# A square root on ScalarE for the first tile, and a new order of work at the start of a norm, mixer and attention kernel

## The chip, the cores and the metric

The kernel runs on one core of one Trainium2 chip. The metric is the device time of one execution in microseconds (us).

## The reference, cut to what matters

```python
def _layernorm(x, axis=-1, eps=1e-05):
    m = jnp.mean(x, axis=axis, keepdims=True)
    v = jnp.var(x, axis=axis, keepdims=True)
    return (x - m) / jnp.sqrt(v + eps)
# x: (1, 2048, 1024) bf16
xn = _layernorm(x)
return x + _A_ref(xn, mem0, Wq, Wk, Wv, Wo, seg_len) + _B_ref(xn, w1, w2, w3, w4)
# _B_ref begins with:  h = gelu(layernorm(xn) @ w1)
```

Everything waits for the norm of x. The kernel cuts the 2048 rows into 16 tiles of 128 rows and starts with branch B: it normalizes a tile twice in one step, transposes it, and multiplies it by w1 (1024 x 1024). The long rest (99% of the time) is dense matrix work.

Of the kernel before, what the change touches and what calls it, by code (L numbers as in the profile page):

```python
# [16 lines left out]
F32 = mybir.dt.float32  # L17
I32 = mybir.dt.int32
ALU = mybir.AluOpType
ACTF = mybir.ActivationFunctionType  # L20
# [3 lines left out]
P = 128  # L24
S = 2048
D = 1024
KT = D // P
# [9 lines left out]
EPS = 1e-5  # L37
# [40 lines left out]
def kernel(  # L78
# [16 lines left out]
    nc = tc.nc  # L95
# [46 lines left out]
    ones_f = cpool.tile([P, 1], F32)  # L142
# [4 lines left out]
    epsa = cpool.tile([P, 2], F32)  # L147
# [46 lines left out]
    with tc.manual_schedule(engines={mybir.EngineType.PE, mybir.EngineType.SP, mybir.EngineType.Pool}), ExitStack() as actx:  # L194
# [6 lines left out]
        with ExitStack() as bctx:  # L201
# [13 lines left out]
            with ExitStack() as hctx:  # L215
# [7 lines left out]
                with ExitStack() as p0:  # L223
                    big = p0.enter_context(tc.tile_pool(name="p0big", bufs=1))
# [4 lines left out]
                    xts = {}  # L229
# [18 lines left out]
                    stats = {}  # L248

                    def norm_stats(n, part=None):  # L250

                        if n >= NT:
                            return
                        xt = xts[n]
                        if n not in stats:
                            stats[n] = [ring.tile(shape, F32, tag=tag, bufs=6, name=f"{tag}{n}") for tag, shape in (("st", [P, 2, 6]), ("mv", [P, 2]), ("ab", [P, 2]), ("rr", [P, 2]), ("nm2", [P, 1]))]
                        st, mv, ab, rr, nm2 = stats[n]
                        if part in (None, 0):
                            nc.vector.bn_stats(st[:, 0, :], xt[:, 0:512])
                        if part == 0:  # L260
                            return
                        nc.vector.bn_stats(st[:, 1, :], xt[:, 512:1024])
                        nc.vector.bn_aggr(mv[:], st[:])
                        nc.vector.scalar_tensor_tensor(ab[:], epsm[:], mv[:, 1:2], epsa[:], op0=ALU.mult, op1=ALU.add)
                        nc.gpsimd.tensor_tensor(rr[:], ab[:], neghalf[:], op=ALU.pow)
                        if n >= NPE:
                            nc.gpsimd.tensor_scalar(nm2[:], mv[:, 0:1], rr[:, 1:2], -1.0, op0=ALU.mult, op1=ALU.mult)

                    def norm2(n, xn2T, jj):
                        st, mv, ab, rr, nm2 = stats[n]  # L270
                        xn2 = ring.tile([P, D], BF16, tag="xn2")
                        if n < NPE:
                            for c in (slice(0, 512), slice(512, 1024)) if n == 0 else (slice(0, 1024),):
                                nc.vector.tensor_scalar(xn2[:, c], xts[n][:, c], mv[:, 0:1], rr[:, 1:2], op0=ALU.subtract, op1=ALU.mult)
                        else:
                            nc.scalar.activation(xn2[:], xts[n][:], ACTF.Identity, bias=nm2[:], scale=rr[:, 1:2])
                            nc.sync.dma_start_transpose(xn2T[:, jj], xn2[:])
                        return xn2
# [11 lines left out]
                    def transposes(xn2, xn2T, jj, half, shared=False):  # L290
                        ps = psum0.tile([P, 4, P], F32, tag="tr")
                        for k in range(4):
                            nc.tensor.matmul(ps[:, k, :], xn2[:, (half * 4 + k) * P:(half * 4 + k + 1) * P], ident[:], start=True, stop=True)
                        if shared:
                            nc.scalar.copy(xn2T[:, jj, half * 4:half * 4 + 2, :], ps[:, 0:2])
                            nc.vector.tensor_copy(xn2T[:, jj, half * 4 + 2:half * 4 + 4, :], ps[:, 2:4])
                        else:
                            nc.scalar.copy(xn2T[:, jj, half * 4:half * 4 + 4, :], ps[:])

                    def stage1_k(xn2T):  # L300

                        pss = [psum.tile([P, 4, P], F32, tag="mm", bufs=4, name=f"ps{i}") for i in range(2)]
                        for k in range(KT):
                            if k == KT - 1:
                                tr(1, 0)
                                tr(1, 1)
                            for co in range(KT):
                                nc.tensor.matmul(pss[co // 4][:, co % 4, :], w1_sb[:, k, co * P:(co + 1) * P], xn2T[:, 0, k, :],
                                                 start=(k == 0 and co % 4 == 0), stop=(k == KT - 1), skip_group_check=True)
                        for i in range(2):  # L310
                            nc.scalar.activation(hTB[:, 4 * i:4 * i + 4, 2:2 + P], pss[i][:], ACTF.Gelu_apprx_tanh)
# [12 lines left out]
                    def xn2T_tile():  # L324
                        return ring.tile([P, 2, KT, P], BF16, tag="xn2T", name="xn2T")
# [2 lines left out]
                    wz = big.tile([P, 512], BF16)  # L328
                    nc.vector.memset(wz[:], 0.0)
                    gtab = big.tile([P, 1], F32)  # L330
                    nc.scalar.activation(gtab[:], ones_f[:], ACTF.Gelu_apprx_tanh)

                    ps = psum.tile([P, 512], F32, tag="mm", bufs=4, name="warm")
                    for i in range(12):
# [3 lines left out]
                    def norm2_of(n):  # L338
                        if n % 2 == 0:
                            tiles2[n] = xn2T_tile()  # L340
                        xn2s[n] = norm2(n, tiles2[n - n % 2], n % 2)

                    def tr(n, half, shared=False):
                        transposes(xn2s[n], tiles2[n - n % 2], n % 2, half, shared)

                    norm_stats(0)
                    norm_stats(1, 0)
                    norm2_of(0)
                    tr(0, 0, True)
                    tr(0, 1, True)  # L350
                    norm_stats(1, 1)
                    nc.gpsimd.memset(hTB[:, :, 0:2], 0.0)
                    nc.gpsimd.memset(hTB[:, :, S + 2:S + 4], 0.0)
                    load_consts(4)
                    for n in range(1, NPE):
                        if n > 1:
                            norm_stats(n + 1, 0)
                        norm2_of(n)
                        norm_stats(n + 1, 1 if n > 1 else None)
                        if n > 1:  # L360
                            norm1(n - 2)
                        if n == 1:
                            stage1_k(tiles2[0])
                        elif n < 4:
                            stage1(n - 1, 1, tiles2[(n - 1) // 2 * 2], {4: [lambda n=n: tr(n, 0)], 5: [lambda n=n: tr(n, 1)]}, (n - 1) % 2)
# [20 lines left out]
                with ExitStack() as p2:  # L386
                    ring = p2.enter_context(tc.tile_pool(name="p2ring", bufs=4))
                    for n in range(NT):
                        x1 = ring.tile([P, D], F32, tag="x1")
                        st = ring.tile([P, 2, 6], F32, tag="st")  # L390
                        for ch in range(2):
                            ps = psum.tile([P, 512], F32, tag="mm", bufs=4)
# [5 lines left out]
                        mv = ring.tile([P, 2], F32, tag="mv")  # L398
# [14 lines left out]
            with ExitStack() as p3:  # L413
                psum3 = p3.enter_context(tc.tile_pool(name="psum3", bufs=2, space=PSUM))
                h3T = p3.enter_context(tc.tile_pool(name="p3h", bufs=1)).tile([P, FT, 512], BF16)
                big = p3.enter_context(tc.tile_pool(name="p3big", bufs=1))
# [115 lines left out]
                for tb in range(4):  # L532
                    depth = 1 if tb < 2 else 2
                    for f in range(FT):
                        ps = psum.tile([P, 512], F32, tag="mm", bufs=4)
# [15 lines left out]
                    for j in range(4):  # L551
                        n = tb * 4 + j
# [7 lines left out]
                        for ch in range(2):  # L560
                            ps = psum.tile([P, 512], F32, tag="mm", bufs=4)
# [21 lines left out]
            for hg in range(8):  # L583
# [6 lines left out]
                for m4 in range(4):  # L590
                    Vs = vsp.tile([P, 4, 512], BF16, tag="Vs")
                    for j in range(4):
                        ps = psum.tile([P, 512], F32, tag="mm", bufs=4)
# [180 lines left out]
        for gi_, group in enumerate(groups):  # L774
# [3 lines left out]
            for hg in range(8):  # L778
# [24 lines left out]
                step = 8 * sum(8 * (B["nb"] / 2400 + 0.0025) for B in Bs) / len(work)  # L803
                step = (step * len(work) + 0.36 * len(work)) / len(work)
# [50 lines left out]
        for i in range(2):  # L855
            ps = psum.tile([P, 512], F32, tag="mm", bufs=4)
# [34 lines left out]
    with tc.If(cond > 0):  # L891
        with ExitStack() as fctx:
# [18 lines left out]
            with tc.For_i(0, NSEG, 1) as i:  # L911
# [6 lines left out]
                for hg in range(8):  # L918
# [8 lines left out]
                    ps = fps.tile([P, 4, L], F32, tag="mm")  # L927
# [4 lines left out]
                    ps = fps.tile([P, 4, L], F32, tag="mm")  # L932
# [4 lines left out]
                    ps = fps.tile([P, 512], F32, tag="mm")  # L937
# [33 lines left out]
                for ch in range(2):  # L971
                    ps = fps.tile([P, 512], F32, tag="op")
# [47 lines left out]
```

## The kernel before: the parts that the change touches

```python
load_x(0)                                  # 256 KB each, on the SyncE queue
for c in range(4):                         # w1 in four pieces of 512 KB, two k each
    nc.sync.dma_start(w1_sb[:, 2*c:2*c+2, :], w1_v[:, 2*c:2*c+2, :])
    if c == 0:
        load_x(1)
for n in range(2, 7):
    load_x(n)
# ... w2 and more x tiles

def norm_stats(n, part=None):              # VectorE statistics, then the power on POOL
    # ...
    if part in (None, 0):
        nc.vector.bn_stats(st[:, 0, :], xt[:, 0:512])
    if part == 0:
        return
    nc.vector.bn_stats(st[:, 1, :], xt[:, 512:1024])
    nc.vector.bn_aggr(mv[:], st[:])
    nc.vector.scalar_tensor_tensor(ab[:], epsm[:], mv[:, 1:2], epsa[:], op0=ALU.mult, op1=ALU.add)
    nc.gpsimd.tensor_tensor(rr[:], ab[:], neghalf[:], op=ALU.pow)      # 1/sqrt

def transposes(xn2, xn2T, jj, half, shared=False):
    # four matmuls with the identity into ps, then the copy to SBUF:
    if shared:                                                          # tile 0 only
        nc.scalar.copy(...first two blocks...)
        nc.vector.tensor_copy(...last two blocks...)
    else:
        nc.scalar.copy(...all four...)

def stage1_k(xn2T):                        # tile 0, k outermost, so it follows w1's pieces
    for k in range(KT):                    # KT = 8
        if k == KT - 1:
            tr(1, 0)                       # tile 1's transposes
            tr(1, 1)
        for co in range(KT):
            nc.tensor.matmul(...)          # 128x128x128
    # ... Gelu

# 12 warm-up matmuls of 128x512, then:
norm_stats(0)
norm_stats(1, 0)
norm2_of(0)                                # xn2 = (x - mean) * rr, in two halves
tr(0, 0, True)
tr(0, 1, True)
norm_stats(1, 1)
# ... then for n = 1, 2, ...: norm, statistics of n + 1, stage 1
```

The stage-1 loop of tile 0 is called "the first stage" below, that of tile 1 "the second stage". Tile 2's transposes come in the middle of the second stage.

## Time and profile before

| | before |
|---|---|
| median when the prediction was made (3 executions) | 1516.68 us (1515.07 to 1517.80) |
| median of 6 executions, the first 3 among them | 1515.14 us (1514.63 to 1517.80) |
| span of the profiled execution | 1512.7 us |
| first norm on VectorE | 6.58 us |
| first transpose on TensorE | 7.03 us |
| first matmul of the first stage | 7.89 us |
| tile 2's transposes | 14.71 us |

The busy shares and the chain of waits of the profile's page of before:

```profile
PE 1502.8 (99%) x9778; PEld 807.9 (53%) x9850; DVE 545.2 (36%) x1138; ACT 504.1 (33%) x1142; POOL 178.9 (12%) x248
...
PE 98%; DMA 1%; issue 0%; ACT 0%; DVE 0%; SPq 0%
```

PE is TensorE, DVE VectorE, ACT ScalarE, POOL GpSimd, and a lower case q behind an engine means its queue of DMA issues. TensorE is the limit nearly everywhere. What TensorE waited for (engine, line, releaser: us in total, number of times, longest):

```profile
...
PE ps L293 <- DVE xn L274: 0.4, 1, 0.4
PE psO L706 <- DMA PT<-Pn: 0.2, 1, 0.2
```

So there is little to win, and nearly all of it lies in the first 13 us. The profile models the end of a matmul with some 0.16 us of draining, so this view understates or omits short waits. Below, "waits of PE" are taken from the starts of consecutive matmuls in the trace, less their normal pitch (56 ns for 128 columns at full clock).

The timeline of before, cut (start, busy us, engine, line, operation, out<-in, count, and in brackets the idle time and what ended it):

```profile
1.38 5.30 PE L335 MATMUL warm<-wz 128*128 128x512 bf16 x12 [1.38 <-DVE wz L329]
...
5.34 0.72 POOL L265 TENSOR_TENSOR rr<-ab,neghalf 128x2 f32<-128x2 f32 x1 [2.73 <-DVE ab L264]
...
5.97 0.69 DVE L259 BATCH_NORM_STATS2 st<-xt 128x6 f32<-128x512 bf16 x1 [0.72 <-DMA xt<-in_A_x_dram]
6.58 0.72 DVE L274 TENSOR_SCALAR xn<-xt,mv,rr 128x512 bf16<-128x512 bf16 x2
...
7.03 0.72 PE L293 MATMUL ps<-c_ident_sb,xn 128*128 128x128 bf16 x8 [0.35 <-DVE xn L274]
...
7.89 3.29 PE L308 MATMUL ps<-xn2T,w_sb 128*128 128x128 bf16 x56
...
11.00 0.69 DVE L259 BATCH_NORM_STATS2 st<-xt 128x6 f32<-128x512 bf16 x1
...
11.14 0.62 PE L293 MATMUL ps<-c_ident_sb,xn 128*128 128x128 bf16 x8
...
12.22 2.66 PE L318 MATMUL ps<-xn2T,w_sb 128*128 128x128 bf16 x40
...
14.71 0.39 PE L293 MATMUL ps<-c_ident_sb,xn 128*128 128x128 bf16 x4
```

POOL is done with the power at 6.06, but VectorE has just begun half of tile 1's statistics (5.97), because x tile 1 landed at 5.94; so the norm of tile 0 runs only at 6.58. TensorE waits 0.13 us before 11.14 for tile 1's norm, 0.17 before 12.22 and 0.27 at the fifth matmul of that group (12.70) for the copies of tile 1. Tile 2's statistics start at 11.00, behind tile 1's norm and without waiting for x tile 2, which the trace shows landing at 10.69. Tile 2's transposes (14.71) wait for nothing.

### The profile page before, as it was taken

The page shows a single profiled execution, that of the slowest core. Times are in us where ns is not written, and L with a number is a line of the kernel's source. Part 1 is how long each engine was busy: PE and PEld are TensorE (multiplying, and loading weights), DVE is VectorE, ACT ScalarE, POOL GpSimd, SP SyncE. Part 2 cuts the span into 40 slices and gives each one's busy share as a digit, 9 for nine tenths or more (in the row PEclk, how much of TensorE's full clock was granted, in tenths as well). Part 3 has the DMA queues.
Part 4 walks back from the last instruction along what each step waited for, and adds up shares of the span by engine and source line. Part 5 has one row for each costly group of instructions (what it writes and reads, how often), then busy time and mean ns, then how long its engine had stood idle before and what let it go on. Part 6 is the DMA issues. An engine that isn't in the chain of part 4 may idle for free.

```text
span 1512.7 us, 24295 instructions
## 1 busy us (share of the span) xinstructions
PE 1502.8 (99%) x9778; PEld 807.9 (53%) x9850; DVE 545.2 (36%) x1138; ACT 504.1 (33%) x1142; POOL 178.9 (12%) x248
## 2 busy tenths in 40 slices
PE   9999999999999999999999999999999999999998
PEld 7844444445444444444466645664665455545555
DVE  8382230100020122222246624651564166516642
ACT  6533203013012011111256614650663266416630
POOL 5231020211111231100000010001000100010001
PEclk9999999999999999999999999999999999999999
DMA  8699762353345887632399947992998299818811
GB/s 295 147 255 334 218 176 91 137 202 112 125 163 145 196 274 253 208 120 84 126 245 242 246 124 183 245 238 71 239 248 203 73 227 224 216 60 212 190 47 52
DMA packets 303539, 274.11 MB, mean 181 GB/s; under 512 B 153926, under 2 KB 270184, under 8 KB 303424
## 3 DMA queue, kind: packets, MB, share of 16 engines
q1 hardware_dynamic: 281248, 189.92, 50.5%
q0 software_dynamic: 22032, 82.54, 15.8%
q8 instruction: 79, 1.29, 0.4%
q14 instruction: 36, 0.29, 0.1%
q10 hardware_dynamic: 144, 0.07, 0.0%
HBM read 190.93 MB, written 46.14 MB: 157 GB/s over the span
## 4 chain that ended last, share of the span: by engine, by line
PE 98%; DMA 1%; issue 0%; ACT 0%; DVE 0%; SPq 0%
PE ps L667 30%; PE pso L725 15%; PE ps L595 15%; PE ps L537 13%; PE ps L563 13%; PE ps L395 4%; PE ps L318 3%; PE psS L682 2%; PE psO L706 2%; PE ps L860 1%; PE ps L487 1%; PE gps L466 0%; PE ps L452 0%; DMA PT<-Pn 0%; DMA xt<-in_A_x_dram 0%
## 5 line engine op out<-in xcount | busy, mean ns | idle before, releaser
L667 PE MATMUL ps<-hTb,wt 128*128 128x396 bf16 (+2 forms) x2528 | 497.5, 343 | 0.0
L667 PEld LDWEIGHTS <-wt 128*128 128x128 bf16 x2528 | 232.8, 98 | 166.4
L595 PE MATMUL ps<-wt,xT 128*128 128x512 bf16 x1003 | 220.1, 379 | 1.1
L725 PE MATMUL pso<-wo_sb,oX 128*128 128x512 bf16 (+1 forms) x972 | 209.3, 372 | 1.1
L537 PE MATMUL ps<-xn3T,w_sb 128*128 128x512 bf16 x896 | 196.2, 379 | 0.0
L563 PE MATMUL ps<-w_sb,h3T 128*128 128x512 bf16 x873 | 194.3, 379 | 1.2
L595 PEld LDWEIGHTS <-xT 128*128 128x128 bf16 x1024 | 100.2, 98 | 120.8
L538 ACT ACTIVATE h3T<-ps 128x512 bf16<-128x512 f32 x112 | 66.8, 597 | 290.4 <-PE ps L537 289.5
L725 PEld LDWEIGHTS <-oX 128*128 128x128 bf16 x992 | 96.1, 98 | 106.5
L673 ACT CAST KT<-ps 128x462 bf16<-128x462 f32 (+2 forms) x160 | 81.9, 512 | 191.0 <-PE ps L667 189.2
L563 PEld LDWEIGHTS <-h3T 128*128 128x128 bf16 x896 | 87.0, 98 | 103.3
L537 PEld LDWEIGHTS <-w_sb 128*128 128x128 bf16 x896 | 86.6, 98 | 102.1
L688 DVE TENSOR_REDUCE sums<-sm 99x4 f32<-99x396 f32 (+2 forms) x176 | 97.6, 555 | 113.2 <-ACT sm L686 113.2
L675 ACT ACTIVATE QT<-ps 128x462 bf16<-128x462 f32 (+2 forms) x160 | 83.9, 525 | 113.1 <-PE ps L667 101.5
L597 ACT CAST Vs<-ps 128x512 bf16<-128x512 f32 x64 | 37.5, 586 | 233.2 <-PE ps L595 174.9
L684 DVE TENSOR_TENSOR sm<-psS,c_mask_reg_sb 99x396 f32<-99x396 f32 x152 | 86.7, 570 | 76.9 <-PE psS L682 76.9
L686 ACT ACTIVATE sm<-sm 99x396 f32<-99x396 f32 (+2 forms) x176 | 92.7, 527 | 59.0 <-DVE sm L684 54.1
L601 DVE CAST Vs<-ps 128x512 bf16<-128x512 f32 x64 | 44.3, 692 | 170.0 <-PE ps L595 160.4
L694 DVE TENSOR_TENSOR Pn<-sm,rs 99x396 bf16<-99x396 f32 (+2 forms) x176 | 98.9, 562 | 7.3 <-DMA PT<-Pn 1.2
L564 DVE TENSOR_TENSOR R<-ps,R 128x512 f32<-128x512 f32 x32 | 21.9, 690 | 180.5 <-PE ps L563 166.3
L732 POOL DMA_DIRECT2D out_dram<-ot x30 | 16.3, 545 | 587.2 <-DVE ot L731 581.4
L731 DVE TENSOR_TENSOR ot<-pso,Rt 128x512 bf16<-128x512 f32 (+1 forms) x33 | 22.3, 675 | 171.7 <-PE pso L725 166.3
(124 smaller groups left out, 1071.5 us busy)
## 6 DMA issues: line engine op xcount, KB each, us to landing
wt<-in_A_Wq_dram SPq DMA_DIRECT2D x76, 512.0 KB
wt<-in_A_Wk_dram SPq DMA_DIRECT2D x76, 512.0 KB
wt<-in_A_Wv_dram POOLq DMA_DIRECT2D x24, 1024.0 KB, 6.6
V_scratch<-Vs SPq DMA_DIRECT2D x32, 512.0 KB
V<-V_scratch SPq DMA_DIRECT2D x40, 384.0 KB
R_scratch<-x POOLq DMA_DIRECT2D x16, 512.0 KB, 5.1
R<-R_scratch SPq DMA_DIRECT2D x16, 512.0 KB
R_scratch<-R POOLq DMA_DIRECT2D x16, 512.0 KB, 3.6
```

Source lines behind the costliest of these rows:

```text
L537: nc.tensor.matmul(ps[:].rearrange("p (n t) -> p n t", t=P), w3_sb[:, k, f * P:(f + 1) * P], xn3T[tb][:, :, k, :], start=(k == 0), stop=(k ...
L538: nc.scalar.activation(h3T[:, f, :], ps[:], ACTF.Gelu_apprx_tanh)
L563: nc.tensor.matmul(ps[:], h3T[:, f, j * P:(j + 1) * P], w4_sb[:, f, ch * 512:(ch + 1) * 512], start=(f == 0), stop=(f == FT - 1))
L595: nc.tensor.matmul(ps[:], xT[:, m4 * 4 + j, k, :], wv[:, k, :], start=(k == 0), stop=(k == KT - 1))
L667: nc.tensor.matmul(ps[:, :nb] if flat else ps[:, :nb].rearrange("p (t c) -> p t c", t=nt), w[:, k, hh * P:(hh + 1) * P], B["rhs"](k), star ...
L673: nc.scalar.copy(o, i)
L675: nc.scalar.mul(o, i, scale)
L684: nc.vector.tensor_tensor(sm[:T, :, :T], S3, t["mask"][:].unsqueeze(1).to_broadcast((T, 4, T)), op=ALU.add)
L686: nc.scalar.activation(e[:T, :, :T], sm[:T, :, :T], ACTF.Exp, scale=LN2)
L688: nc.vector.tensor_reduce(ss, e[:T, :, :T], axis=AX.X, op=ALU.add)
L694: nc.vector.tensor_tensor(Pn[:T, :, :T], e[:T, :, :T], rs[:T, :].unsqueeze(2).to_broadcast((T, 4, T)), op=ALU.mult)
L725: nc.tensor.matmul(self.ps[:, :self.w], self.oX[0][:, h, self.oX[1] + self.gl * P:self.oX[1] + (self.gl + 1) * P], wo_sb[:, h, self.cc], s ...
```

## The change

The intent: get tile 0's scale from a square root on ScalarE and a reciprocal on VectorE, not from POOL; norm tile 0 before any statistics of tile 1; leave tile 0's copies to ScalarE alone; and issue tile 1's transposes one k sooner, so that two steps of matmuls hide their copies. The price is a second load of ScalarE's activation table, as the square root and Gelu belong to different sets (the changed trace has that load at 5.48 us, between the two).

```diff
@@ norm_stats
                         nc.vector.bn_aggr(mv[:], st[:])
+                        if n == 0:
+                            return
+                        scales(n)
+                    def scales(n):
                         nc.vector.scalar_tensor_tensor(ab[:], epsm[:], mv[:, 1:2], epsa[:], ...)
                         nc.gpsimd.tensor_tensor(rr[:], ab[:], neghalf[:], op=ALU.pow)
@@ norm2
-  ... mv[:, 0:1], rr[:, 1:2], ...
+  ... mv[:, 0:1], sd0[:, 1:2] if n == 0 else rr[:, 1:2], ...
@@ transposes
-                        if shared:
-                            nc.scalar.copy(...first two...)
-                            nc.vector.tensor_copy(...last two...)
-                        else:
-                            nc.scalar.copy(...all four...)
+                        step = 2 if shared else 4
+                        for i in range(0, 4, step):
+                            nc.scalar.copy(...blocks i to i + step...)
@@ stage1_k
-                            if k == KT - 1:
+                            if k == KT - 2:
                                 tr(1, 0)
@@ start
-                    nc.scalar.activation(gtab[:], ones_f[:], ACTF.Gelu_apprx_tanh)
+                    nc.scalar.activation(gtab[:], ones_f[:], ACTF.Sqrt)
 ...
                     norm_stats(0)
-                    norm_stats(1, 0)
+                    sd0 = big.tile([P, 2], F32)
+                    nc.scalar.activation(sd0[:, 0:1], stats[0][1][:, 1:2], ACTF.Sqrt, bias=epsa[:, 1:2], scale=1.0 + EPS)
+                    nc.vector.reciprocal(sd0[:, 1:2], sd0[:, 0:1])
                     norm2_of(0)
+                    scales(0)
+                    nc.scalar.activation(gtab[:], ones_f[:], ACTF.Gelu_apprx_tanh)
                     tr(0, 0, True)
                     tr(0, 1, True)
-                    norm_stats(1, 1)
+                    norm_stats(1)
```

No DMA is added, removed or reordered.

More of the change, by code (lines that the diff above doesn't have):

```diff
@@ L263, in norm_stats @@
                         nc.vector.bn_aggr(mv[:], st[:])
+                        if n == 0:
+                            return
+                        scales(n)
+                    def scales(n):
+                        st, mv, ab, rr, nm2 = stats[n]
                         nc.vector.scalar_tensor_tensor(ab[:], epsm[:], mv[:, 1:2], epsa[:], op0=ALU.mult, op1=ALU.add)
@@ L273, in norm2 @@
                             for c in (slice(0, 512), slice(512, 1024)) if n == 0 else (slice(0, 1024),):
-                                nc.vector.tensor_scalar(xn2[:, c], xts[n][:, c], mv[:, 0:1], rr[:, 1:2], op0=ALU.subtract, op1=ALU.mult)
+                                nc.vector.tensor_scalar(xn2[:, c], xts[n][:, c], mv[:, 0:1], sd0[:, 1:2] if n == 0 else rr[:, 1:2], op0=ALU.subtract, op1=ALU.mult)
                         else:
@@ L293, in transposes @@
                             nc.tensor.matmul(ps[:, k, :], xn2[:, (half * 4 + k) * P:(half * 4 + k + 1) * P], ident[:], start=True, stop=True)
-                        if shared:
-                            nc.scalar.copy(xn2T[:, jj, half * 4:half * 4 + 2, :], ps[:, 0:2])
-                            nc.vector.tensor_copy(xn2T[:, jj, half * 4 + 2:half * 4 + 4, :], ps[:, 2:4])
-                        else:
-                            nc.scalar.copy(xn2T[:, jj, half * 4:half * 4 + 4, :], ps[:])
+                        step = 2 if shared else 4
+                        for i in range(0, 4, step):
+                            nc.scalar.copy(xn2T[:, jj, half * 4 + i:half * 4 + i + step, :], ps[:, i:i + step])
                     def stage1_k(xn2T):
```

## The prediction

> **What bounds the kernel now.** TensorE: busy 1502.8 of 1512.7 us (first table of the page); the chain of waits is 98% PE. By the starts of consecutive matmuls in the trace, PE truly waits about 0.3 us after 26 us (once, for PT at 797 us). The change touches the first 15 us, so it can win only the few waits there.
>
> **The start, from the timeline of before.** The first x tile lands at 3.44; statistics to 4.99; ab 5.03; POOL's power 5.34 to 6.06; but VectorE has meanwhile begun 0.69 us of statistics of tile 1 (5.97), so the first norm's halves run at 6.58 and 6.89. The twelve warm-up matmuls (427 ns apart) end their issue near 6.47; the first transpose starts at 7.03, its copies at 7.47, stage 1's first matmul at 7.89. PE waits 0.13 us before tile 1's transposes (11.15), 0.17 before the second stage (12.22) and 0.27 in it (12.70, second copy). Tile 2's transposes start at 14.71 without a wait.
>
> **Costs and moves.**
> - Off tile 0's path go ab (0.22), the power (0.72, plus hand-overs) and half statistics of tile 1. On come a 128x1 ScalarE op (about 0.23, after the 0.20 of the table-warming one) and a 128x1 VectorE reciprocal (about 0.2): xn2's first half at about 6.0 in place of 6.98.
> - PE can't use all of that: the warm-up holds it to about 6.47, and the first transposes then run at half clock (until about 7 us). They end near 7.1 in place of 7.43: 0.35 us won.
> - ScalarE loads a table again behind the root. In the Trainium skill, "ScalarE: Activation LUTs", section "What ACT_TABLE_LOAD costs", a switch is 1283 ns plus a drain of about 1380. This trace shows 1283 ns twice, each time with the next activation 11 ns later: no further drain. So 5.29 to 6.79 with the activation behind it, free before the copies at 7.1.
> - Copies: four of 372 ns on ScalarE, 0.32 apart; stage 1 takes 0.45 us for each k, two per copy: nothing waits. VectorE loses 0.76 us of copies.
> - Tile 1's norm is done near 9.65 in place of 11.09. Transposes one step (0.45 us) sooner hide their copies behind two k steps: the waits 0.13 + 0.17 + 0.27 go.
>
> Sum 0.92 us. But tile 2's x lands only at 10.69. From its statistics to its norm's end the trace shows 3.2 us, so xn2 of tile 2 is ready near 13.95, and PE arrives near 13.8: 0.15-0.2 given back. Net gain **about 0.75 us**, 0.05%.
>
> **Time.** 1516.68 minus 0.75, and the four known executions of before average 0.6 below the median: **1515.6 us**, range 1513.6 to 1517.6. Faster by over 2% 0.003, within 2% 0.994, slower 0.003. Three runs of before spread over 2.7 us, so the gain will barely show in the times, only in the trace.
>
> **If right, the profile shows** the first norm at about 5.6; the first transpose near 6.5, directly behind the warm-up, at doubled pitch until the clock rises; stage 1's first matmul near 7.5; a table load at 5.3 of 1.28 us; no wait around tile 1's transposes; the second stage starting near 11.55; a new short wait of PE for xn2 before tile 2's transposes, which start near 13.95 in place of 14.71; later PE work shifted by 0.7-0.8 us.
>
> **What would make it wrong.** A drain around the second table load (copies at 8 us: a loss of about 0.2). The clock rising at another moment. x tiles or w1 pieces landing earlier or later (w1's last lands at 10.01, needed at 10.65). A later wait that takes the shift back.

## The result, and the profile after

| | before | changed |
|---|---|---|
| median of 6 executions | 1515.14 us (1514.63 to 1517.80) | 1515.41 us (1514.31 to 1516.37) |
| span of the profiled execution | 1512.7 us | 1513.3 us |
| first norm | 6.58 | 5.70 |
| first transpose | 7.03 | 6.17 |
| first matmul of the first stage | 7.89 | 7.29 |
| statistics of tile 2 start | 11.00 | 11.62 |
| tile 2's transposes | 14.71 | 14.85 |

The ratio is 0.9998, with a 95% interval of 0.9985 to 1.0011: the same. That interval is about 4 us wide around a predicted effect of 0.75 us, so the times cannot judge the prediction; the trace has to.

The page of the changed kernel (its lines are numbered 4 to 8 higher from the start section on; L299 is L293 of before, L312 is L308, L322 is L318, L280 is L274):

```profile
PE 1506.1 (100%) x9850; PEld 807.6 (53%) x9850; DVE 544.3 (36%) x1137; ACT 506.4 (33%) x1147; POOL 178.9 (12%) x248
...
PE 98%; DMA 1%; ACT 0%; DVE 0%; SPq 0%; issue 0%; POOL 0%
```

PE's busy time is not comparable here: the trace of before lacks 72 matmul records (9778 against 9850). What TensorE waited for in the changed kernel:

```profile
...
PE ps L299 <- DVE xn L280: 0.6, 1, 0.6
PE ps L312 <- ACT xn2T L302: 0.4, 1, 0.4
PE psO L714 <- DMA PT<-Pn: 0.3, 1, 0.3
PE ps L312 <- DMA w_sb<-in_B_w_dram: 0.3, 1, 0.3
```

The wait for xn (VectorE's norm) is no longer that of tile 0 but one in front of tile 2's transposes, and a wait for a piece of w1 is new. The timeline of the changed kernel, cut as that of before:

```profile
1.38 4.65 PE L339 MATMUL warm<-wz 128*128 128x512 bf16 x12 [1.38 <-DVE wz L333]
...
5.17 0.30 ACT L352 ACTIVATE sd<-mv,epsa 128x1 f32<-128x1 f32 x1 [2.92 <-DVE mv L263]
5.48 1.28 ACT L356 ACT_TABLE_LOAD   x1
...
5.70 0.74 DVE L280 TENSOR_SCALAR xn<-xt,mv,sd 128x512 bf16<-128x512 bf16 x2
...
6.17 0.72 PE L299 MATMUL ps<-c_ident_sb,xn 128*128 128x128 bf16 x8
...
6.78 0.20 ACT L356 ACTIVATE gtab<-ones_f 128x1 f32<-128x1 f32 x1
6.88 1.17 ACT L302 CAST xn2T<-ps 128x256 bf16<-128x256 f32 x4
6.91 0.69 DVE L259 BATCH_NORM_STATS2 st<-xt 128x6 f32<-128x512 bf16 x1 [0.35 <-DMA xt<-in_A_x_dram]
7.29 2.02 PE L312 MATMUL ps<-xn2T,w_sb 128*128 128x128 bf16 x32 [0.40 <-ACT xn2T L302]
...
9.62 1.07 PE L312 MATMUL ps<-xn2T,w_sb 128*128 128x128 bf16 x16 [0.31 <-DMA w_sb<-in_B_w_dram]
...
10.53 0.61 PE L299 MATMUL ps<-c_ident_sb,xn 128*128 128x128 bf16 x8
...
11.62 0.69 DVE L259 BATCH_NORM_STATS2 st<-xt 128x6 f32<-128x512 bf16 x1 [1.56 <-DMA xt<-in_A_x_dram]
...
11.87 2.40 PE L322 MATMUL ps<-xn2T,w_sb 128*128 128x128 bf16 x40
...
14.85 0.40 PE L299 MATMUL ps<-c_ident_sb,xn 128*128 128x128 bf16 x4 [0.59 <-DVE xn L280]
```

TensorE gains as hoped at first: the fifth matmul of the second stage starts at 12.09 against 12.70, 0.61 us sooner, although a wait of 0.47 us for w1's third piece has come in before 9.62. Then it stands still for 0.75 us (its last matmul would have been followed at 14.10; the brackets say 0.59 because the drain counts as busy). The chain of waits of the changed kernel's start, in order of time (start, us, what), says what it stood still for:

```profile
3.70 7.89 DMA xt<-in_A_x_dram
...
11.62 0.69 DVE st L259
12.31 0.60 DVE st L262
...
13.49 0.73 POOL rr L271
...
14.25 0.56 DVE xn L280
...
14.85 0.40 PE ps L299 x4
```

The start now hangs on the landing of x tile 2 at 11.60, then 3.23 us of statistics, power and norm. In before's profile that tile landed at 10.69. So 0.61 us were won and 0.75 given back. The span grew by 0.6, not by 0.14: the rest is mostly the wait for PT near 798 us (0.49 against 0.33) and another at 860 us (0.25, new); the first of these came out between 0.33 and 0.65 us over all profiles, whatever the kernel.

### The profile page after: what moved, and what is told of

It is laid out like the page before. It is cut to its first block, busy times and chain, and to the rows that moved or that the text cites. A ratio compares the mean times of both kernels' runs of the same rounds, so it can differ in the third digit from the quotient of the medians.

```text
span 1513.3 us, 24372 instructions
## 1 busy us (share of the span) xinstructions
PE 1506.1 (100%) x9850; PEld 807.6 (53%) x9850; DVE 544.3 (36%) x1137; ACT 506.4 (33%) x1147; POOL 178.9 (12%) x248
## 4 chain that ended last, share of the span: by engine, by line
PE 98%; DMA 1%; ACT 0%; DVE 0%; SPq 0%; issue 0%; POOL 0%
PE ps L675 30%; PE pso L733 15%; PE ps L603 15%; PE ps L545 13%; PE ps L571 13%; PE ps L403 4%; PE ps L322 3%; PE psS L690 2%; PE psO L714 2%; PE ps L868 1%; PE ps L495 1%; DMA xt<-in_A_x_dram 1%; PE gps L474 0%; PE ps L460 0%; DMA PT<-Pn 0%; ACT xn2T L302 0%
```

## The experiments

Theory A: the loads come late by chance, and x tile 2 is what bounds the changed start. Theory B: the change itself delays the loads. Runs that start with a_ are the changed kernel with an edit, those with b_ the kernel before with one; diffs are against that kernel. This table holds the readings of all profiles, in us. "Loads" is the landing of the last of tile 1, w1's four pieces and tile 2; "gap" is tile 2's transposes less the start of its statistics.

| run | clock to full | first norm | first transpose | loads | tile 2's statistics | tile 2's transposes | gap |
|---|---|---|---|---|---|---|---|
| before | 6.96 | 6.58 | 7.03 | 10.69 | 11.00 | 14.71 | 3.71 |
| b_again | 7.23 | 6.57 | 7.03 | 10.68 | 11.08 | 14.79 | 3.71 |
| changed | 5.24 | 5.70 | 6.17 | 11.60 | 11.62 | 14.85 | 3.23 |
| a_again | 6.87 | 5.57 | 6.47 | 11.68 | 11.70 | 14.93 | 3.23 |
| a_third | 6.69 | 5.78 | 6.47 | 11.65 | 11.67 | 14.90 | 3.23 |
| a_table_late | 7.01 | 5.55 | 6.47 | 11.13 | 11.15 | 14.38 | 3.23 |
| a_tr_last | 6.85 | 5.73 | 6.47 | 11.33 | 11.35 | 14.71 | 3.36 |
| a_pow | 5.91 | 6.07 | 6.54 | 10.83 | 10.86 | 14.08 | 3.22 |
| b_tr_sooner | 5.87 | 6.73 | 7.18 | 10.84 | 11.15 | 14.88 | 3.73 |
| a_x2_early | 6.09 | 5.60 | 6.29 | 10.63 | 9.44 | 13.82 | 4.38 |
| a_x2_again | 4.37 | 5.66 | 6.13 | 10.70 | 9.50 | 13.89 | 4.39 |
| a_pow_x2 | 4.27 | 6.25 | 6.72 | 11.76 | 10.43 | 14.95 | 4.52 |
| b_x2_early | 4.49, lost at 7.91 | 7.19 | 7.64 | 11.26 | 11.81 | 16.51 | 4.70 |
| b_warm8 | 12.76 | 6.46 | 6.91 | 11.44 | 11.46 | 16.92 | 5.46 |

### b_again, a_again and a_third: the two kernels unchanged

The edits: none.

> The kernel before, unchanged: a null for the times and a second draw of when the x tiles land. Theory A (landing by chance): tile 2's x lands anywhere in 10.6 to 11.6 us, and tile 2's transposes start at the later of two things: PE's own arrival (about 14.7) and the start of tile 2's statistics on VectorE plus 3.25 us. Theory B (the change itself delays the loads): statistics of tile 2 here again near 11.0, as in the first profile of before. Ratio to before: 1.000, interval about 0.1% each way.

> The changed kernel, unchanged: a second draw. Theory A: the start of tile 2's statistics lies anywhere in 10.6 to 11.6 us, and tile 2's transposes start 3.25 us after it (13.9 to 14.9), PE waiting for it, except where PE itself comes later (about 13.5 to 13.8 at the earliest). Theory B: statistics of tile 2 start again near 11.6, transposes again near 14.85, so no gain at all. Ratio to before 0.9995 (A) or 1.000 (B): the times will not tell these apart.

> The changed kernel, unchanged, a third draw. Tile 2's transposes 3.23 us behind the start of tile 2's statistics, as in the four runs with this order so far (or at PE's own arrival, about 13.7, if that is later). If the late loads belong to this program, statistics start again at 11.6 to 11.7; if they come by chance, anywhere from 10.7 on. Ratio to before 0.9995 to 1.0005.

Times: b_again 1515.25 us median, 5 runs, ratio 1.0005 (0.9991 to 1.0019); a_again 1515.29, 5 runs, 0.9999 (0.9985 to 1.0012), before of the same rounds being 1515.13; a_third 1515.13, 5 runs, 0.9998 (0.9985 to 1.0011), before 1515.31. The changed kernel is the same as before in three sets of rounds.

All three profiles of the changed kernel have tile 2's transposes 3.23 us behind the start of tile 2's statistics, and its statistics start 0.02 us behind x tile 2's landing. Both profiles of before land at 10.7, all three of the changed kernel at 11.6 to 11.7. Chance, as theory A has it, looks poor: the landing seems to belong to the program. But in a_third x tile 1 came on time (5.85) and the delay arose later, at w1's second piece, while in a_again x tile 1 was already 1.04 us late (6.98).

### a_x2_early, a_x2_again: x tile 2 loaded ahead of w1's last piece

```diff
                     for c in range(4):
                         nc.sync.dma_start(w1_sb[:, 2 * c:2 * c + 2, :], w1_v[:, 2 * c:2 * c + 2, :])
-                        if c == 0:
-                            load_x(1)
-                    for n in range(2, 7):
+                        if c in (0, 2):
+                            load_x(1 + c // 2)
+                    for n in range(3, 7):
```

> The changed kernel with the load of x tile 2 moved ahead of w1's last piece. If tile 2's x is what bounds the changed start (theory A), its statistics start behind tile 1's norm (about 9.7 to 10.3), xn2 of tile 2 is ready by about 13.0 to 13.5, and PE does not wait for it: transposes of tile 2 at PE's own arrival, 13.8 to 14.2 with w1's last piece landing at 10.7 to 11.6 (a wait for that piece of up to 0.6 us may appear in stage 1 before its last two k). If something else on PE's side bounded it, the transposes stay at 14.7 to 14.9. Ratio 0.999 to 1.000.

> The changed kernel with tile 2's x loaded ahead of w1's last piece, a second draw. Tile 2's transposes at PE's own arrival, with no wait for xn2, 13.8 if w1's last piece lands at 10.6 and up to 0.9 later if the loads are late by as much. Median again below that of before of the same rounds, by 0.3 to 1.0 us; the interval of the ratio will still hold 1.

Tile 2's transposes came at 13.82 and 13.89, with no wait for xn. The timeline of a_x2_early, cut:

```profile
9.44 0.69 DVE L259 BATCH_NORM_STATS2 st<-xt 128x6 f32<-128x512 bf16 x1
...
10.68 1.07 PE L312 MATMUL ps<-xn2T,w_sb 128*128 128x128 bf16 x16 [0.20 <-DMA w_sb<-in_B_w_dram]
...
13.82 0.39 PE L299 MATMUL ps<-c_ident_sb,xn 128*128 128x128 bf16 x4
```

The wait has moved to w1's last piece (0.36 us by the starts of matmuls). The span fell to 1511.9 us, 0.77 below before's for a shift of 0.89 in tile 2's transposes: here the shift at the start reached the end. In a_x2_again tile 2's transposes came 0.82 us sooner but the span (1512.3 us) fell by only 0.35: longer waits for transfers near 790 us (0.17, new) and 798 us (0.60 against 0.33) took the rest. These two kernels do on the core what the change meant to do, and here the loads were on time. In times it hardly shows: a_x2_early 1514.46 us (5 runs) against 1515.13, ratio 0.9997 (0.9983 to 1.0011); a_x2_again 1515.15 (6 runs, one of them at 1524.21) against 1515.31, ratio 1.0012 (0.9994 to 1.0030). The second median missed the 0.3 us that was expected.

The program still holds the square root and the table load at 5.39, and yet its loads are on time. So theory B in the form "the table load delays the DMAs" falls. How busy the queues were, in a view by stretches (stretch, length, busy time and count for PE, PEld, DVE, ACT, POOL, then granted clock, DMA share, GB/s), of before, of the changed kernel and of a_x2_early:

```profile
4.50:8.00 3.50, 3.01 (x16) 1.07 (x14) 2.14 (x7) 0.53 (x2) 0.72 (x1) 1.00 1.05 391
```

```profile
4.50:8.00 3.50, 2.96 (x27) 1.58 (x25) 2.72 (x8) 2.80 (x7) 0.72 (x1) 1.00 0.96 338
```

```profile
4.50:8.00 3.50, 3.20 (x29) 1.84 (x27) 3.00 (x10) 2.86 (x7) 0.72 (x1) 1.00 1.03 386
```

The changed kernel moved 338 GB/s where the others moved 391 and 386. Its trace shows single packets of 2 KB there that took up to 0.46 us, most packets taking 0.08. Behind the first rush of loads, whose last slow packet ended between 3.4 and 4.2 us in all runs, they begin at 4.54, before the square root (5.17) and the table load (5.48).

The traces say a little more of the lateness. The load of x tile 2 was issued at 3.68 us in before and at 3.70 in the changed kernel, so the delay arises after the issue. A landing is reported in 16 parts, and only the last few of them are late: in the changed kernel 15 of the 16 parts of x tile 2 had landed by 11.01, the last at 11.60. Between 4.3 and 8 us the four profiles whose loads landed by 10.70 (before, b_again, a_x2_early, a_x2_again) have none, 1, 3 and 1 packets of over 0.2 us; the ten others, with landings at 10.83 to 11.76, have 7 to 23. Among these ten are b_x2_early and b_warm8, which hold no part of the change.

### b_x2_early: the same move in the kernel before

The same edit as above, in the kernel before.

> The kernel before with the same move of the load. Theory A says that its tile 2 transposes were bound by PE's own work, not by tile 2's x, so they stay at about 14.7 (a little later if w1's last piece comes late), although tile 2's statistics can start no sooner than behind tile 1's norm (about 11.0). If tile 2's x bounded both kernels, it would come forward by up to 0.5 us.

A miss, and an instructive one: 16.51 in place of 14.7. x tile 1 landed at 6.55 here, so its statistics (6.58), which stand in front of the first norm in this kernel, pushed that to 7.19. The clock had risen early (4.49), so the warm-up was over by 5.66 and TensorE stood idle for 1.98 us. Then the clock was taken back for one window. The stretches of b_x2_early:

```profile
4.49:7.91 3.42, 1.44 (x10) 0.53 (x8) 2.02 (x6) 0.00 (x0) 0.72 (x1) 1.00 1.01 366
7.91:11.32 3.41, 3.41 (x34) 3.26 (x32) 1.88 (x5) 0.74 (x2) 0.71 (x3) 0.50 1.05 402
```

Granted 0.50 for 3.41 us, which at half rate loses at most about 1.7 us (half of 3.41). The edit itself can't be judged from this run. In a_pow_x2 (below) the clock rose nearly as early (4.27) and stayed, with TensorE busy for 2.10 us of the next stretch where it was busy for 1.44 here:

```profile
4.27:7.68 3.41, 2.10 (x16) 0.99 (x15) 2.50 (x8) 0.52 (x2) 0.72 (x1) 1.00 1.00 363
```

### b_warm8: the kernel before with 8 warm-up matmuls

```diff
-                    for i in range(12):
-                        nc.tensor.matmul(ps[:], wz[:, :P], wz[:], start=(i == 0), stop=(i == 11))
+                    for i in range(8):
+                        nc.tensor.matmul(ps[:], wz[:, :P], wz[:], start=(i == 0), stop=(i == 7))
```

> The kernel before with 8 warm-up matmuls in place of 12: the idle time of PE in front of the first transpose grows from about 0.6 to 2.2 us. If idle time there can cost the clock (as one run, with 2 us of it, showed: granted half again for 3.4 us), the clock is low for part or all of stage 1's first tile in most executions, and the median rises by 0.7 to 1.7 us, tile 2's transposes at 15.5 to 16.5. If idle time costs only itself, nothing changes: the first norm is still at 6.6, tile 2's transposes at 14.7 and the ratio 1.000.

The executions were 1514.38, 1515.78, 1517.46, 1517.49 and 1517.96 us (median 1517.46) against 1515.31; the ratio, 1.0007 (0.9994 to 1.0020), does not confirm a slowdown, though the median lies 2.15 us higher. In the profiled one, of 1517.49, tile 2's transposes came at 16.92, later than the 15.5 to 16.5 expected. Its timeline:

```profile
6.91 1.03 PE L293 MATMUL ps<-c_ident_sb,xn 128*128 128x128 bf16 x8 [1.94 <-DVE xn L274]
...
7.98 5.55 PE L308 MATMUL ps<-xn2T,w_sb 128*128 128x128 bf16 x56
```

The 56 matmuls took 5.55 us, 99 ns each, where before took 3.29: the clock was half until 12.76. (The clock column of the page counts time before the first clock record as 1.00; the pitch of the matmuls is the better witness there.) So idle time of TensorE in front of the first norm can go with a loss of clock, not only of itself: in b_x2_early the clock had risen and was taken back, here it had not risen before 12.76. A shorter warm-up and a longer idle time are one and the same edit, so this run doesn't tell them apart. The executions fall into two groups, near 1515 and near 1517.5. Before had two executions above 1517 (1517.80, 1517.52) among 32 over all rounds; the changed kernel had none among 16, at most 1516.37. That the changed kernel is safer against this fall-back is plausible, as it shortens that idle time, but two in 32 against none in 16 is not a proof.

### a_pow: no square root, the order alone

```diff
-                    nc.scalar.activation(gtab[:], ones_f[:], ACTF.Sqrt)
+                    nc.scalar.activation(gtab[:], ones_f[:], ACTF.Gelu_apprx_tanh)
 ...
                     norm_stats(0)
-                    # square root, reciprocal, norm2_of(0), scales(0), Gelu table
+                    scales(0)
+                    norm2_of(0)
```

> The changed kernel without the square root on ScalarE and without a second table load: tile 0's scale comes from the power on POOL as in before, but tile 1's statistics stay behind the first norm. The first norm starts about 6.1 to 6.25 (root: 5.6 to 5.7; before: 6.6), so about half of the gain at the first norm is the order alone; first transpose at about 6.6 (root: 6.2 to 6.5). Tile 2's transposes: no later than with the root by more than 0.1 us, if tile 2's x bounds them. Theory B by the table load: statistics of tile 2 near 11.0.

The first norm ran at 6.07, without any ScalarE work. Of the 0.88 us that the changed kernel won at the first norm (6.58 to 5.70), 0.51 came with the order alone (single profiles; x tile 0 landed at 3.44 in before, 3.58 in the changed kernel and 3.42 here). The first transpose was at 6.54, against 6.13 to 6.47 with the root. Tile 2's x came at 10.83 here, so tile 2's transposes came at 14.08, 0.63 us before those of before: with the landing near that of before's profile, the predicted gain is nearly there, without the square root. TensorE was ready at 13.64 and waited 0.44 us for tile 2's norm, so a sooner first norm could have won nothing here. Statistics near 11.0 without the table load are also what theory B expected of this run; taken alone it doesn't decide. The timeline of a_pow, cut:

```profile
6.07 0.73 DVE L280 TENSOR_SCALAR xn<-xt,mv,rr 128x512 bf16<-128x512 bf16 x2 [0.84 <-POOL rr L271]
...
10.86 0.69 DVE L259 BATCH_NORM_STATS2 st<-xt 128x6 f32<-128x512 bf16 x1 [0.99 <-DMA xt<-in_A_x_dram]
...
14.08 0.40 PE L299 MATMUL ps<-c_ident_sb,xn 128*128 128x128 bf16 x4 [0.28 <-DVE xn L280]
```

Its one execution took 1514.23 us, before's beside it 1515.29; single runs carry no weight at this size.

### a_pow_x2: a_pow with x tile 2 loaded early

Both edits together.

> As the one with the early load, but with POOL's power in place of ScalarE's root and without the second table load. If the root is worth nothing once the loads bound the start, tile 2's transposes come within 0.15 us of those with the root at equal landing of w1's last piece (13.8 at 10.6), although the first norm runs 0.4 us later (6.1). Median within 0.5 us of the one with the root.

14.95 in place of 13.8, because w1's last piece landed at 11.76, not 10.63: 1.13 us later for transposes 1.13 us later than in a_x2_early. So with this order the start hangs on w1's last piece in the same way. This program has neither root nor second table load, and its loads are the latest of all: theory B by the table load falls from this side too. Median 1514.36 us (5 runs) against 1515.31, ratio 0.9994 (0.9981 to 1.0007), the lowest ratio of all, and still the same as before. Against a_x2_again of the same rounds (1515.15) it lies 0.79 us lower, where 0.5 was the most expected.

### a_table_late: the Gelu table loaded behind tile 0's copies

```diff
                     scales(0)
-                    nc.scalar.activation(gtab[:], ones_f[:], ACTF.Gelu_apprx_tanh)
                     tr(0, 0, True)
                     tr(0, 1, True)
+                    nc.scalar.activation(gtab[:], ones_f[:], ACTF.Gelu_apprx_tanh)
```

> The changed kernel with the second table load (Gelu) moved behind tile 0's four copies on ScalarE. If the load sits on the path, the first copy starts 0.04 us behind the fourth transpose (6.4 to 7.1 us by the clock's phase), not behind the load, and stage 1's first matmul 0.3 us sooner where the clock rose early. Theory A (tile 2's x lands late by chance and bounds the start): tile 2's transposes still start 3.25 us behind the start of tile 2's statistics, so nothing is won at the end. Theory B (the change's table load at 5.5 us delays the loads): tile 2's statistics start near 11.0 here, as in both profiles of before.

```profile
6.47 0.87 PE L299 MATMUL ps<-c_ident_sb,xn 128*128 128x128 bf16 x8
...
7.15 1.20 ACT L302 CAST xn2T<-ps 128x256 bf16<-128x256 f32 x4 [1.83 <-PE ps L299]
...
8.36 1.28 ACT L358 ACT_TABLE_LOAD   x1
```

That is its timeline, cut. The copies follow the transposes and the load fits into idle time. But the clock rose late (7.01), so the transposes ran slowly, and the load would not have been in their way either: in a_again, with the clock at 6.87, the load and its activation had ended at 6.85, before the fourth transpose (7.06), and the copies started at 7.09. In the profile of the changed kernel, with the clock at 5.24, the fourth transpose ended at 6.56 and the first copy started at 6.88, just behind the load. So the load can cost about 0.3 us there, but this run did not test it. Tile 2's statistics started at 11.15 and its transposes 3.23 us later, as theory A has it. A landing at 11.13 lies between the two kernels', so it doesn't decide for theory B or against it. One execution: 1514.57 us.

### a_tr_last: tile 1's transposes back at the last k

```diff
-                            if k == KT - 2:
+                            if k == KT - 1:
```

> The changed kernel with tile 1's transposes back before the last k. The waits around the second stage come back: about 0.17 us before it and 0.27 before its fifth matmul, as in before. If tile 2's x bounds the start (statistics at 11.6 or so), these waits only eat idle time and tile 2's transposes stay 3.25 us behind the start of its statistics; if it lands at 10.7, they cost up to 0.3 us. Theory B: statistics of tile 2 near 11.6 again; theory A: anywhere from 10.7 to 11.7.

The waits of before came back, 0.17 us before the second stage and 0.27 at its fifth matmul. Tile 2's transposes came 3.36 us behind its statistics, by 0.13 later than x tile 2 asked for: they were bound by TensorE's own arrival again, as in before. By this count, an estimate from this one profile, the sooner transposes would have been worth 0.13 us at this landing (11.33), nothing at about 11.5 or later, more at an earlier one. One execution: 1516.06 us.

### b_tr_sooner: the sooner transposes alone, in the kernel before

The reverse edit in the kernel before.

> The kernel before with only tile 1's transposes one k sooner. PE now gets to them at about 10.6 but tile 1's norm is ready only at 11.1, so PE waits about 0.5 us; the waits of 0.17 and 0.27 around the second stage go. Net: tile 2's transposes at 14.7, as before: this part alone wins nothing. Statistics of tile 2 near 11.0.

TensorE waited 0.58 us for tile 1's norm (its transposes at 11.29), and the two later waits were gone. Tile 2's transposes at 14.88, not sooner than before's 14.71 and 14.79. This part pays only where the norm of tile 1 comes sooner as well. One execution: 1514.87 us.

## Why the prediction was right or wrong

**The time.** 1515.6 us predicted, 1515.41 measured, within the range. This is no proof of the sum: the median of before, over six executions, was 1515.14 and not 1516.68, so the predicted gain of 0.75 us is not in the times. That the number came so close is luck: a baseline that was too high made up for the gain that did not come. Three sets of rounds gave ratios of 0.9998, 0.9999 and 0.9998. The prediction had said that a gain would barely show there.

**The front of the chain: right up to the first stage.** The first norm at about 5.6 came at 5.70, 5.57 and 5.78. Where the clock rose late (6.87, 6.69), the first transpose came at 6.47 behind the warm-up and the first stage at 7.52 and 7.43, as forecast; in the profile of the result the clock rose at 5.24 and they came at 6.17 and 7.29. The waits around tile 1's transposes went.

**The table load: right in its cost.** The Trainium skill, page "ScalarE: Activation LUTs", section "What ACT_TABLE_LOAD costs", has 1283 ns for the load and about 1380 ns of drain. The load took 1283 ns (5.482 to 6.765); the square root had ended 18 ns before it, and the next activation started at 6.776, 11 ns behind it: no drain of that kind. That ScalarE would be "free before the copies" held only for the late clock; with the early one the load held the first copy by about 0.3 us.

**The failed step: "0.15-0.2 given back".** The mechanism is in the prediction, named as a new wait before tile 2's transposes, and its length of 3.2 us from the start of the statistics was borne out: 3.22 or 3.23 to tile 2's transposes in every profile bound by it. What was mis-sized is the landing of x tile 2: 10.69, read from one profile of before. The prediction lists another landing among its risks, but gives it no size; all three profiles of the changed kernel show 11.60 to 11.68. The term measured 0.75. A second, smaller term was missing: 0.47 us of waiting for w1's third piece (9.58 in place of 8.66), which would have cost something even with x tile 2 on time: the second stage started at 11.87 to 11.96 and not near 11.55, and TensorE was ready for tile 2 at 14.10 and not near 13.8. The sum for the profile is then 0.61 won and 0.75 given back; the predicted "0.7-0.8" of shift in all later work was a loss of 0.14.

**What is shown and what stays open.** Shown: with that load order the changed start is bound by the landing of x tile 2 (3.22 or 3.23 us in five profiles, from 10.86 to 11.70), and loading it sooner brings tile 2's transposes 0.9 us ahead of before's (13.82 and 13.89 against 14.71 and 14.79) as long as w1's last piece is on time (a_pow_x2, where it was not: 14.95). Shown: the lateness needs neither the square root nor the table load, as a_x2_early and a_x2_again have both and were on time, and a_pow_x2 has neither and was latest. Nor is it the chip: a_again and a_x2_early ran on one, a_third and a_x2_again on another. Not shown: that the square root won anything at the end, as a_pow came to tile 2 at 14.08 without it. Open: why one program's loads come on time and another's up to 1.1 us late. It looks tied to the build, because before (10.69, 10.68), the changed kernel (11.60, 11.68, 11.65) and the kernel of a_x2_early (10.63, 10.70) each repeated themselves within 0.1; no run tells what in the build does it. That speaks against theory A's word "by chance", but seven profiles don't refute it.

## What to carry to other kernels

When the head of a kernel is shortened, list for each wait how late its data may come before it binds: here the slack in front of tile 2 fell from about 0.5 us (xn2 ready at 14.20 for transposes at 14.71) to less than nothing, so the start passed from the engines to the loads, and a difference of 0.9 us in a landing took everything. Read landings from several profiles before building on them, and when a computation moves forward move its load forward too. An expected gain below the spread of the times can be judged only by marks in the trace.

## What the Trainium skill lacked or had wrong

- "ScalarE: Activation LUTs", section "What ACT_TABLE_LOAD costs": it gives 1283 ns and about 1380 ns of drain for every switch of sets. The load agrees to the nanosecond; 18 ns passed before it and 11 ns behind it, so no run here shows the drain.
- "ScalarE: Activation LUTs", section "Table sets: the hidden batching unit": it says that cheap functions such as copy are in every set. a_table_late agrees: its four copies ran with the square root's table, 1.20 us together, and no load came before them.
- "TensorE: Matmul & The Clock Gate", Part 1: it describes a free-running window of 3413 ns, and one run agrees with its length (clock changes at 4.49, 7.91 and 11.32 us, so 3.42 and 3.41 apart); that the clock rose anywhere from 4.27 to 7.23 us behind one and the same warm-up fits the rest. It gives the rule that idle gaps of more than about 3.4 us cost the clock, and tells, without a length or a share, of frequent short ones that did. In b_x2_early a gap of 1.98 us was enough, in a window in which PE was busy for 1.44 of 3.42 us; in a_pow_x2, busy for 2.10 of 3.41 us with a gap of 1.17, the clock stayed. The page lacks the busy share that a window needs; these two runs don't fix it either.
- No page that was consulted has it that early loads of one and the same order may land up to 1.1 us later in one build of a kernel than in another (10.63 to 11.76 us here), and that this repeated from run to run. In the changed kernel one of the 16 parts of x tile 2's load came 0.59 us behind the rest (11.60 against 11.01).
